# Where six groups of values products of a pair of heads stand in TensorE's order

## The chip, the cores and the metric

The kernel runs on one core of a Trainium2 chip. The metric is the device time of one execution in microseconds (us).

## The reference

Three layers follow each other; only the first is touched. It is attention over 2 x 8 heads of 768 rows and 64 columns in which a query sees a key only if both fall into the same of 16 clusters of their head:

```
q_assign, k_assign = argmax over clusters of normalised q, k against centroids
scores = scale * q @ k.T, masked to q_assign == k_assign
attn = softmax(scores);  attn_out = attn @ v
x = attn_out as 1536 rows of 512
x = sum over 4 experts of p_e * (relu(x @ w1[e]) @ w2[e])
out = leaky_relu(x @ w_in) @ w_out
```

## The kernel before

The 16 heads t = 0 to 15 are worked one after the other, as 8 pairs (an even t and the odd t after it). Every head is cut into six blocks of 128 rows. These are the pieces of work that matter, each with its lines:

- **M(t, j)**, `emit_M`, L509: the scores of one block of queries in a short form, two matmuls (L515) into a 1024-column PSUM tile, and on VectorE (DVE) the largest of each row (L519).
- **E(t, j)**, `emit_E`, L545: the scores of one block of keys against all queries, four matmuls (L550, L551), and on ScalarE (ACT) the exponential of them (L553).
- **P(t, j)**, `emit_P`, L555: the exponentials split into a high f16 part phi (L561 on DVE or L563 on ACT) and a rest plo (L564, on GpSimd, which is POOL, for nearly all).
- **V(t, j)**, `emit_V`, L568: the values products of one block of queries: 18 short f16 matmuls (L576 to L578) of 64 or 65 columns. It reads all of phi and plo of head t and writes the head's own `small` PSUM tile. TensorE (PE) alone works in it. A V group stands about one head behind the E of its head.
- Preparation of a pair to come: transposes T (two per pair, one for q and one for k, L335, split by ACT and DVE, L139 and L140), the similarities simT and sims (L349, L361), the argmax on DVE (L382 to L386), of which L382 and L383 read the sims out of PSUM, and the transpose ohT (L406).
- X of a finished pair: six transposes (L604), split by ACT and DVE (L139, L140). Single transposes mrow (L534) and vall (L458).

M, E, T, simT, sims, ohT, mrow, vall and X take their PSUM tile from one ring of three, `big()` (L126). So each of them can begin only when the reader of the piece that took its tile three pieces earlier is done with it. V takes none of the three.

The order of the work is written out by hand: `at(when, ...)` (L866) gives each piece a place in units of one E, and L959 sorts them by it. `V_AT` (L23) has the places of V(t, 0) to V(t, 5), the first tuple for even heads and the second for odd ones, counted from the start of the following head (L881). Heads 14 and 15 use `V_LAST` instead. Every engine works off its instructions in the order so made.

Of the kernel before, what the change touches and what calls it, by code (L numbers as in the profile page):

```python
# [19 lines left out]
PHI_ON_VECTOR = ((0, 2, 5), (3,))  # L20
PLO_ON_VECTOR = (13, 5)
M_AT = ((1.25, 2.08, 2.35, 3.21, 5.26, 5.79), (0.67, 1.9, 2.06, 2.76, 4.04, 5.42))
V_AT = ((1.84, 2.15, 2.31, 3.56, 4.97, 5.13), (1.44, 2.97, 3.24, 4.31, 4.57, 5.82))  # L23
NORM_AT = (6.53, 6.12)
PREP_V_AT = (2.41, 2.77)
MROW_AT = (1.43, 1.0)
# [49 lines left out]
def attention_moe_kernel(  # L76
# [789 lines left out]
    def at(when, fn, *args):  # L866
        line.append((when, len(line), fn, args))

    for t in range(NH):
# [8 lines left out]
        for j in range(J):  # L878
            if t > 1:
                at(o - 2 * J + M_AT[par][j] if t > 3 else (M2_AT, M3_AT)[t - 2][j], emit_M, t, j)  # L880
            at(o + J + (V_AT if t < NH - 2 else V_LAST)[par][j], emit_V, t, j)  # L881
        at(o + J + (NORM_AT if t < NH - 2 else NORM_LAST)[par], emit_norm, t)
# [551 lines left out]
```

## Time and profile before

| | |
|---|---|
| time, median of 3 (lowest to highest) | 965.48 us (965.24 to 966.52) |
| the profiled execution's own time | 967.07 us |
| its span | 965.4 us |
| PE busy, over the span | 946.0 us (98%) |
| DVE, ACT, POOL busy | 743.8, 518.7, 552.5 us |
| granted TensorE clock | 1.00 |

The attention stage is the first quarter of the span; heads 2 to 13 run from about 59 to 218 us. In the timeline views a row has the start in us, how long the row lasts, the engine, the line, the operation, what is written and read, its shape and how many follow at once. A bracket gives the idle time before it and what ended it. Matmuls overlap each other in these rows, so the time that a piece takes on PE is read as its start to the next piece's start, and a short wait can stand there with no bracket.

### The profile page before, as it was taken

The page shows a single profiled execution, that of the slowest core. Times are in us where ns is not written, and L with a number is a line of the kernel's source. Part 1 is how long each engine was busy: PE and PEld are TensorE (multiplying, and loading weights), DVE is VectorE, ACT ScalarE, POOL GpSimd, SP SyncE. Part 2 cuts the span into 40 slices and gives each one's busy share as a digit, 9 for nine tenths or more (in the row PEclk, how much of TensorE's full clock was granted, in tenths as well). Part 3 has the DMA queues.
Part 4 walks back from the last instruction along what each step waited for, and adds up shares of the span by engine and source line. Part 5 has one row for each costly group of instructions (what it writes and reads, how often), then busy time and mean ns, then how long its engine had stood idle before and what let it go on. Part 6 is the DMA issues. An engine that isn't in the chain of part 4 may idle for free.

```text
span 965.4 us, 16126 instructions
## 1 busy us (share of the span) xinstructions
PE 946.0 (98%) x6339; PEld 545.3 (56%) x6372; DVE 743.8 (77%) x1263; ACT 518.7 (54%) x733; POOL 552.5 (57%) x443
## 2 busy tenths in 40 slices
PE   8899999999999999999999999999999999999998
PEld 5688888887544455555555555555544444444443
DVE  6989998889687766666766666766889997877764
ACT  3677777779434444334344344344486565555642
POOL 4477777780345665455655465654536666676661
PEclk9999999999999999999999999999999999999999
DMA  7775567550111012110211102103101221221003
GB/s 168 181 177 129 127 136 157 118 136 5 44 44 44 23 37 63 44 44 23 66 33 45 44 29 71 44 22 131 68 21 46 87 87 44 88 88 59 29 1 131
DMA packets 59540, 70.80 MB, mean 73 GB/s; under 512 B 25060, under 2 KB 42088, under 8 KB 59464
## 3 DMA queue, kind: packets, MB, share of 16 engines
q1 hardware_dynamic: 59464, 69.77, 26.7%
q8 instruction: 50, 0.82, 0.4%
q14 instruction: 26, 0.21, 0.1%
HBM read 46.19 MB, written 3.17 MB: 51 GB/s over the span
## 4 chain that ended last, share of the span: by engine, by line
PE 78%; DVE 15%; ACT 3%; issue 2%; DMA 1%; POOL 1%; SPq 0%; DVEq 0%; ACTq 0%
PE z L1064 22%; PE z L1194 8%; PE z L1195 7%; PE z L1196 7%; PE z L1075 5%; PE z L1252 4%; PE z L1254 3%; PE z L1253 3%; PE big L515 3%; PE z L1123 3%; DVE m L519 2%; PE big L550 2%; PE big L551 2%; DVE acc L1204 1%; PE small L576 1%
## 5 line engine op out<-in xcount | busy, mean ns | idle before, releaser
L140 POOL TENSOR_TENSOR hlo<-g,hhi 128x512 bf16<-128x512 f32 x140 | 194.4, 1407 | 93.0 <-ACT hhi L139 93.0
L1204 DVE SCALAR_TENSOR_TENSOR acc<-z,outer,acc 128x512 f32<-128x512 f32 x180 | 133.8, 747 | 63.3 <-PE z L1196 63.0
L564 POOL TENSOR_TENSOR plo<-p,phi 128x768 f16<-128x768 f32 x83 | 136.1, 1652 | 72.8 <-ACT phi L563 43.1
L139 ACT ACTIVATE hhi<-g 128x512 f16<-128x512 f32 x140 | 86.8, 628 | 119.3 <-DVE g L797 117.8
L1194 PE MATMUL z<-hhi,w2hi 128*128 128x512 f16 x384 | 145.5, 379 | 1.6
L1195 PE MATMUL z<-hhi,w2lo 128*128 128x512 f16 x384 | 145.5, 379 | 0.0
L267 POOL TENSOR_TENSOR w2lo<-w2raw,w2hi 128x512 f16<-128x512 f32 x46 | 57.2, 1264 | 134.2 <-ACT w2hi L264 134.2
L1196 PE MATMUL z<-hlo,w2hi 128*128 128x512 bf16 x353 | 133.8, 379 | 0.0
L519 DVE TENSOR_REDUCE m<-big 128x1 f32<-128x768 f32 x96 | 89.9, 950 | 13.8 <-PE big L515 13.6
L553 ACT ACTIVATE p<-big 128x768 f32<-128x768 f32 x96 | 76.6, 808 | 33.7 <-PE big L551 28.3
L267 POOL TENSOR_TENSOR w1lo<-w1raw,w1hi 128x512 f16<-128x512 f32 x46 | 55.8, 1234 | 41.6 <-ACT w1hi L264 22.1
L1103 DVE TENSOR_TENSOR part<-z,part 128x512 f32<-128x512 f32 (+1 forms) x62 | 34.8, 578 | 53.9 <-PE z L1064 39.6
L1261 DVE SCALAR_TENSOR_TENSOR accn<-z,outer,accn 128x512 f32<-128x512 f32 x84 | 60.4, 744 | 20.5 <-PE z L1254 20.0
L1075 PE MATMUL z<-xx,w1hi 128*128 128x512 f16 x256 | 76.2, 379 | 0.0
L1252 PE MATMUL z<-w2hi,hhi 128*128 128x512 f16 x192 | 72.8, 379 | 0.1
L1254 PE MATMUL z<-w2hi,hlo 128*128 128x512 f16 x192 | 72.8, 379 | 0.0
L1253 PE MATMUL z<-w2lo,hhi 128*128 128x512 f16 x192 | 72.8, 379 | 0.0
L550 PE MATMUL big<-qka 128*128 128x512 f32 x192 | 70.1, 367 | 2.8 <-DVE m L519 1.2
L797 DVE SCALAR_TENSOR_TENSOR g<-z,pb 128x512 f32<-128x512 f32 x92 | 52.5, 576 | 24.3 <-PE z L1064 10.1
L1064 PEld LDWEIGHTS <-shi 128*128 128x128 f16 x496 | 48.5, 98 | 37.1 <-issue 0.7
L578 PE MATMUL small<-vt,plo 128*128 128x65 f16 x576 | 61.2, 192 | 2.2 <-DVE plo L564 1.6
L1196 PEld LDWEIGHTS <-w2hi 128*128 128x128 f16 x384 | 37.6, 98 | 45.3
(247 smaller groups left out, 2301.5 us busy)
## 6 DMA issues: line engine op xcount, KB each, us to landing
qkb<-pair SPq DMA_DIRECT2D x32, 384.0 KB
w1raw<-in_moe_w_dram SPq DMA_DIRECT2D x16, 512.0 KB
w2raw<-in_moe_w_dram SPq DMA_DIRECT2D x16, 512.0 KB
w1raw<-in_moe_w_in_dram SPq DMA_DIRECT2D x8, 1024.0 KB
w2raw<-in_moe_w_out_dram SPq DMA_DIRECT2D x8, 1024.0 KB
qka<-pair SPq DMA_DIRECT2D x16, 384.0 KB
vraw<-in_v_dram SPq DMA_DIRECT2D x16, 192.0 KB
pb<-pe_rows SPq DMA_DIRECT2D x4, 768.0 KB
```

Source lines behind the costliest of these rows:

```text
L140: lo_engine.tensor_tensor(out=lo, in0=src, in1=as_read(hi), op=ALU.subtract)
L267: nc.gpsimd.tensor_tensor(out=lo[:, x], in0=src[:, x], in1=hi[:, x], op=ALU.subtract)
L519: nc.vector.tensor_reduce(out=m_t[t][:, j:j + 1], in_=ps[:, 0:S], op=ALU.max, axis=AX.X)
L564: (nc.vector if plo_on_vector else nc.gpsimd).tensor_tensor(out=plo, in0=p, in1=phi, op=ALU.subtract)
L1064: nc.tensor.matmul(ps, lhsT=w[i][:, k, :], rhs=x[j][:, k, sub], start=first and k + i + j == 0, stop=k == 1 and i == 1, skip_group_check=True,
L1075: nc.tensor.matmul(like(ps, rhs), lhsT=w[:, k, fs], rhs=rhs, start=k + i == 0, stop=k == KC - 1 and i == 2,)
L1194: nc.tensor.matmul(out, lhsT=whi[:, f, ks], rhs=h, start=f == 0, stop=False)
L1195: nc.tensor.matmul(out, lhsT=wlo[:, f, ks], rhs=h, start=False, stop=False)
L1196: nc.tensor.matmul(out, lhsT=whi[:, f, ks], rhs=l, start=False, stop=f == NF - 1)
L1204: nc.vector.scalar_tensor_tensor(out=a, in0=out, scalar=by, in1=a, op0=ALU.mult, op1=ALU.add)
L1252: nc.tensor.matmul(ps, lhsT=hi[:, f, ts], rhs=whi[:, f, :], start=f == 0, stop=False)
L1253: nc.tensor.matmul(ps, lhsT=hi[:, f, ts], rhs=wlo[:, f, :], start=False, stop=False)
```

## The change

Four numbers of `V_AT` are changed; nothing else is.

```
-V_AT = ((1.84, 2.15, 2.31, 3.56, 4.97, 5.13), (1.44, 2.97, 3.24, 4.31, 4.57, 5.82))
+V_AT = ((2.14, 2.15, 2.31, 3.56, 5.12, 5.13), (1.44, 3.58, 3.59, 4.31, 4.57, 5.82))
```

For heads 0 to 13 this changes the order on PE at three places of a pair. With heads 8 and 9 as the example (pieces on PE only; the ring's tile is taken by all but V):

```
place 1 (even head)
before: sims, E(9,1), mrow, V(8,0), M(11,1), E(9,2), M(11,2), V(8,1), V(8,2), M(11,3)
after:  sims, E(9,1), mrow, M(11,1), E(9,2), M(11,2), V(8,0), V(8,1), V(8,2), M(11,3)
place 2 (even head)
before: E(9,4), M(11,4), X, V(8,4), E(9,5), V(8,5), M(11,5)
after:  E(9,4), M(11,4), X, E(9,5), V(8,4), V(8,5), M(11,5)
place 3 (odd head)
before: E(10,2), M(12,1), M(12,2), V(9,1), E(10,3), M(12,3), T(7,0), V(9,2), T(7,1), E(10,4)
after:  E(10,2), M(12,1), M(12,2), E(10,3), M(12,3), T(7,0), T(7,1), V(9,1), V(9,2), E(10,4)
```

No instruction is added or removed, and no other engine's own order changes, since a V group has none but PE's instructions.

## Rows read from the trace of the kernel before

**Rows 1.** Busy time by stretch, one pair: stretch, length, each engine

```profile
core 0: us, PE busy (x) PEld busy (x) DVE busy (x) ACT busy (x) POOL busy (x), PEclk, DMA share, GB/s
...
168.80:195.60 26.80, 26.38 (x337) 23.10 (x335) 23.75 (x38) 20.97 (x30) 19.69 (x13) 1.00 0.51 112
```

**Rows 2.** Chain of waits, 164 to 172 us: start, us on the chain, engine, tile, line

```profile
167.60 0.96 DVE m L519
...
169.45 1.13 DVE phi L561
...
171.50 0.62 PE big L515 x2
```

**Rows 3.** Timeline of PE around place 1 of heads 8 and 9

```profile
157.75 0.19 PE L576 MATMUL small<-vt,phi 128*128 128x65 f16 x1
...
158.27 0.19 PE L578 MATMUL small<-vt,plo 128*128 128x65 f16 x1
158.47 0.59 PE L515 MATMUL big<-qka 96*128 96x512 f32 x2
158.90 0.40 PE L550 MATMUL big<-qka 128*128 128x512 f32 x1
...
159.61 0.51 PE L515 MATMUL big<-qka 96*128 96x512 f32 x2
159.95 0.21 PE L576 MATMUL small<-vt,phi 128*128 128x65 f16 x1
...
160.51 0.19 PE L576 MATMUL small<-vt,phi 128*128 128x65 f16 x1
```

**Rows 4.** Timeline of PE around place 3 of heads 9 and 10

```profile
172.32 0.20 PE L576 MATMUL small<-vt,phi 128*128 128x65 f16 x1
...
172.88 0.48 PE L550 MATMUL big<-qka 128*128 128x512 f32 x1
...
173.66 0.52 PE L515 MATMUL big<-qka 96*128 96x512 f32 x2
174.03 0.88 PE L335 MATMUL big<-ident,qraw 128*128 128x128 f32 x6
174.74 0.19 PE L576 MATMUL small<-vt,phi 128*128 128x65 f16 x1
...
175.30 0.85 PE L335 MATMUL big<-ident,kraw 128*128 128x128 f32 x6
175.91 0.48 PE L550 MATMUL big<-qka 128*128 128x512 f32 x1
```

**Rows 5.** Timeline of DVE at place 1 of heads 8 and 9

```profile
157.76 0.56 DVE L383 TENSOR_TENSOR eq<-big,mx 128x384 bf16<-128x384 f32 x1
```

**Rows 6.** Timeline of PE, place 1 of heads 4 and 5

```profile
104.53 0.59 PE L515 MATMUL big<-qka 96*128 96x512 f32 x2 [0.32 <-DVE eq L383]
```

**Rows 7.** Line L383, 59 to 245 us: count, ns, first and last start

```profile
L383 DVE TENSOR_TENSOR eq<-big,mx x5: 557/558/559, 76.1 to 184.6; 128x384 bf16<-128x384 f32 x5
```

**Rows 8.** Timeline of DVE, place 1 of heads 12 and 13

```profile
208.48 0.95 DVE L519 TENSOR_REDUCE m<-big 128x1 f32<-128x768 f32 x1
```

**Rows 9.** Timeline of POOL after place 2: plo of block 5 of head 9

```profile
168.51 1.65 POOL L564 TENSOR_TENSOR plo<-p,phi 128x768 f16<-128x768 f32 x1
```

**Rows 10.** Timeline of ACT at place 3: the exponential of E(10, 2)

```profile
171.33 0.81 ACT L553 ACTIVATE p<-big 128x768 f32<-128x768 f32 x1 [0.56 <-PE big L551]
```

**Rows 11.** Timeline of DVE at place 3: the maxima of M(12, 1), M(12, 2)

```profile
172.15 1.82 DVE L519 TENSOR_REDUCE m<-big 128x1 f32<-128x768 f32 x2
```

**Rows 12.** Groups of PE instructions, 59 to 245 us: count, busy us, mean ns

```profile
L335 PE MATMUL big<-ident,qraw 128*128 128x128 f32 x30 | 4.4, 282 | 0.0
```

**Rows 13.** Timeline of DVE, place 3 of heads 11 and 12

```profile
198.97 1.82 DVE L519 TENSOR_REDUCE m<-big 128x1 f32<-128x768 f32 x2
```

**Rows 14.** Timeline of PE at place 2 of heads 8 and 9: X, E(9, 5)

```profile
164.42 0.82 PE L604 MATMUL big<-ident,xn 128*128 128x128 f32 x6
...
165.63 0.48 PE L550 MATMUL big<-qka 128*128 128x512 f32 x1
```

**Rows 15.** Timeline of ACT at place 2: the exponential of E(9, 4)

```profile
164.33 0.81 ACT L553 ACTIVATE p<-big 128x768 f32<-128x768 f32 x1 [0.19 <-PE big L551]
```

## The prediction

> **What bounds the kernel now.** I read the page first, then the busy time by stretch, then the timeline of PE, and for every short wait of PE the timeline of the engine that ends it. In the attention stage a pair of heads takes about 26.8 us, of which PE is busy for 26.38; DVE has 23.75, ACT 20.97 and POOL 19.69, and the granted clock is 1.00 throughout [rows 1]. So what a pair costs is PE's own work plus a few waits that hardly show. The chain of waits says where they lie: it runs along PE except at one point of a pair, where it goes from a row maximum over the conversion to phi and the next maximum to the M that waited for its PSUM tile [rows 2]. Two more waits stand in the timeline with no bracket, and the change touches both.
>
> **What a join can save.** An E that follows an M takes 0.71 us to the next piece (158.90 to 159.61) [rows 3]; one that follows a V group takes 0.78 (172.88 to 173.66) [rows 4]. An M after V takes 0.43 (158.47 to 158.90), after E 0.34 (159.61 to 159.95) [rows 3]. So each passage from short f16 matmuls back to f32 ones costs 0.07 to 0.09 us. Three passages a pair over seven pairs would be 21 x 0.08 = 1.7 us. At place 2 nothing of it is real: X is a run of short transposes too, and there E follows X where it followed V, with the same passage bounded by 0 and 0.09.
>
> The Trainium skill (TensorE: Matmul & The Clock Gate, Architectural detail: the array is 16× 32×32, not 1× 128×128) says that TensorE's queue can pull a weight load ahead of matmuls that still run. By that rule the passage is free, and a join saves 0 instead of 1.7 us; the rows above, 0.78 against 0.71, do not agree with it in full.
>
> **Place 1.** V(8,0) runs from 157.75, its last matmul starts at 158.27, and M(11,1) starts at 158.47 [rows 3]. A V group takes 0.56 (159.95 to 160.51) [rows 3], so PE was free at 158.31 and waited 0.16. The reason: the ring gives M(11,1) the tile of sims, three pieces earlier, and sims is read last by L383 on DVE, which ends at 157.76 + 0.56 = 158.32 [rows 5]. For heads 4 and 5 the view names this releaser itself, with 0.32 of idle PE [rows 6]. So V(8,0) is what PE does while DVE still holds the tile. After the change PE comes to M(11,1) at 157.75, and the tile is still not free before 158.47, since nothing that L383 waits for has moved: 0.72 us of idle PE. M(11,1), E(9,2) and M(11,2) then run as before, and V(8,0) is added ahead of V(8,1). M(11,3) starts a whole V group later: +0.56, at most +0.59 if M's own first load is no longer behind the V, and no less than +0.48 if the passage saved by the join is all kept. I take 0.56. Behind the waiting M stand E(9,2) and all later PE work; V matmuls cannot step past it.
>
> L383 is there five times, from 76.1 to 184.6 us, for heads 2, 4, 6, 8 and 10 [rows 7]. For head 12 there are no sims, and the ring gives M(15,1) the tile of M(15,0), whose maximum ends at 208.48 + 0.95 = 209.43 [rows 8]; the same wait. Six times 0.56 = 3.4 us. Head 0 lies among the waits of the start: between 0 and 0.56, I take 0.2.
>
> Does the delay reach the end? From M(11,3) to X PE has no wait, so X comes 0.56 later; ACT's split of X, phi of block 4, then plo on POOL follow in order, and POOL's last plo ends at 168.51 + 1.65 = 170.16 [rows 9], just before the conversion that the chain passes at 169.45 + 1.13 = 170.58 [rows 2]. Both ways, over POOL and over the maxima, begin behind the added group, so M(12,1) at 171.50 moves by the same amount.
>
> **Place 3.** V(9,1) runs from 172.32 to 172.88, then E(10,3), M(12,3) at 173.66, and T(7,0) at 174.03 [rows 4]. After the change E(10,3) comes at 172.32; its tile was E(10,2)'s, read by ACT until 171.33 + 0.81 = 172.14 [rows 10], so it need not wait. M(12,3) would come at 172.32 + 0.71 = 173.03, but takes the tile of M(12,1), and T(7,0) that of M(12,2). Both maxima stand as one row on DVE, 172.15 + 1.82 = 173.97 [rows 11]. M(12,1)'s half ends near 173.1; M(12,2)'s ends at 173.97, 0.06 before T(7,0) started. So T(7,0) cannot come sooner than 174.03: the 0.56 of V(9,1) and the 0.07 of the passage turn into idle PE. T(7,0) takes 0.71 (174.03 to 174.74) and T(7,1) 0.61 (175.30 to 175.91) [rows 4]; a T straight after a T stands nowhere, and I bound it by 0.61 and 0.71. Then V(9,1), V(9,2) at 0.56 each. E(10,4) comes at 174.03 + 0.71 + 0.61 to 0.71 + 1.12 = 176.47 to 176.57, against 175.91: +0.56 to +0.66. I take 0.56, a V group, as at place 1. T(7,1) does come earlier, by 0.56, but its split on ACT and DVE is waited for by nobody near.
>
> The q transposes count 30 in this stretch, six to a head: five heads, 1, 3, 5, 7 and 9 [rows 12]; 5 x 0.56 = 2.8 us. Head 11 has no T; M(14,3) then waits for the first half of 198.97 + 1.82 [rows 13], about the 0.07 to 0.13 that is left after the join: 0.1. Head 13 has no M and no T there: 0 to -0.08, I take 0. From E(10,4) to the next maximum wait PE is without waits, so this too goes through.
>
> **Place 2.** X takes 164.42 to about 165.08; E(9,5) would come then instead of at 165.63 [rows 14]. Its tile is E(9,4)'s, read until 164.33 + 0.81 = 165.14 [rows 15]: 0.06 to 0.12 of wait, and up to 0.09 for the passage. So M(11,5) comes 0 to 0.2 later. The conversion that follows ends only behind POOL's 170.16 [rows 9], which does not depend on place 2; I take 0, and 6 x 0.2 = 1.2 us if that cover is not there.
>
> **Sum.** 3.4 + 0.2 + 2.8 + 0.1 + 0 = 6.5 us. The profiled execution took 967.07 us (span 965.4, and 1.7 around it); it would become 973.6. The median of the runs is 965.48, 1.6 lower; the same 6.5 on it gives 972.0.
>
> **Rivals.** (a) The tiles come free earlier than I read them: the 0.16 before M(11,1) has no bracket, and T(7,0) shows no wait at all. Then all three joins keep their passage: 965.48 - 1.7 = 963.8, not slower. It decides if L383 releases before 157.75, or M(12,2)'s maximum before 173.4. Against it: both starts follow the DVE rows by 0.15 and 0.06, and the row of heads 4 and 5 names L383 [rows 6]. By the rule of the Trainium skill cited above (a) would come to 965.5. (b) Place 1 is absorbed: M(12,1) waited for DVE in any case [rows 2], and if that wait hangs on something older than X, the later PE only uses it up. 965.48 + 6.5 - 3.4 = 969.1 or, with head 0, 968.9. Against it: everything on that chain I could follow begins behind the added V. (c) Place 2 is not covered either: 972.0 + 1.2 = 973.2. For it: the chain view puts the maximum of M(11,5) on its way [rows 2].
>
> **Chances.** The forecast, both places pay: 0.66, with 970.5 to 973 of its own; (c) 0.10; (b) 0.12; (a) 0.12, of which a third is faster by over 0.2%, and two thirds are within it. About 0.2% (1.9 us) is what a measurement of this kernel can tell from no change. Slower 0.88, same 0.08, faster 0.04. The range goes from 968.0, under (b), to 974.0, over (c); it leaves out (a) and some of the rest.
>
> **What would show it.** After the change: M(11,1) (first of two L515 behind the single L534) with about 0.7 us of idle PE that DVE's L383 ends, in five pairs, and for head 12 one that L519 ends; T(7,0) with some 0.4 us that L519 ends; the pair at 27.9 instead of 26.8 us, with PE's busy time unchanged or a little lower, and the feed-forward part as long as before. If M(11,1) comes within 0.2 us behind mrow, place 1 was misread; if T(7,0) starts under 0.2 us behind M(12,3)'s end, place 3 was. If both idle times are there and the pair is not longer, the delay was taken back behind M(12,1) or in the last two heads, and the sum is wrong in what reaches the end.

## The result, and the profile after

The changed kernel takes 971.92 us (median of 6 runs, 971.19 to 973.18) against 965.36 for the kernel before beside it (6 runs, 965.17 to 966.66): ratio 1.0063 [1.0053, 1.0074], slower, and 0.1 us from the forecast. That closeness is partly luck: executions of either kernel differ by up to 2 us in their start-up (E(1,0) starts between 42.4 and 44.3 us in the traces), and three of the six runs of after, against two of the six of before, are over 1 us longer than the rest. So from here on I compare by place: how much later a PE instruction starts than in the kernel before, counted from the start of E(1,0), which stands ahead of every changed place. For this the two ends of the attention stage, of PE's timeline before and after:

```profile
44.33 0.40 PE L550 MATMUL big<-qka 128*128 128x512 f32 x1
...
247.87 0.82 PE L604 MATMUL big<-ident,xn 128*128 128x128 f32 x6
```

```profile
42.45 0.40 PE L550 MATMUL big<-qka 128*128 128x512 f32 x1
...
252.01 0.82 PE L604 MATMUL big<-ident,xn 128*128 128x128 f32 x6
```

From E(1,0) to X(7) it is 203.54 us before and 209.56 after: the attention stage is 6.0 us longer. The shortest runs of the two, 971.19 and 965.17, lie as far apart. The profiled execution of after started 1.88 us earlier in this count, and took 971.24 us where the one of before took 967.07: 4.17, which is 6.02 - 1.88 within 0.03. The feed-forward part behind it is as long as it was: 717.5 us from X(7) to the end of the span in both.

The stretch of one pair, which answers to [rows 1] (stretch, length, busy time of each engine):

```profile
core 0: us, PE busy (x) PEld busy (x) DVE busy (x) ACT busy (x) POOL busy (x), PEclk, DMA share, GB/s
171.22:199.20 27.98, 26.87 (x337) 23.02 (x335) 23.23 (x38) 21.14 (x30) 19.76 (x13) 1.00 0.49 108
```

The pair went from 26.80 to 27.98, with the same 337 matmuls and the same clock. PE's busy time rose by 0.49, though it does nothing more: this is waiting that the profile draws as work. Two rows below show it. The single L534 is drawn 0.27 long, and the M behind it came 0.03 later where its tile was free (e5 below); M(12,3) is drawn 0.62 long, and took 0.37 before.

PE around place 1 of heads 8 and 9, as [rows 3], and DVE there, as [rows 5]:

```profile
159.36 0.27 PE L534 MATMUL big<-ident,m 128*6 128x128 f32 x1
160.20 0.59 PE L515 MATMUL big<-qka 96*128 96x512 f32 x2 [0.56 <-DVE eq L383]
...
161.33 0.51 PE L515 MATMUL big<-qka 96*128 96x512 f32 x2
161.69 0.21 PE L576 MATMUL small<-vt,phi 128*128 128x65 f16 x1
...
162.80 0.19 PE L576 MATMUL small<-vt,phi 128*128 128x65 f16 x1
```

```profile
159.49 0.56 DVE L383 TENSOR_TENSOR eq<-big,mx 128x384 bf16<-128x384 f32 x1
```

L383 ends at 160.05, and M(11,1) starts 0.15 behind it: the same 0.15 as before, but now with nothing between L534 and M(11,1). Then come E(9,2), M(11,2) and three V groups in a row (161.69 to 163.35) instead of two.

PE around place 3 of heads 9 and 10, as [rows 4], and DVE there, as [rows 11]:

```profile
174.61 0.50 PE L550 MATMUL big<-qka 128*128 128x512 f32 x1
...
175.46 0.62 PE L515 MATMUL big<-qka 96*128 96x512 f32 x2
176.32 0.88 PE L335 MATMUL big<-ident,qraw 128*128 128x128 f32 x6 [0.25 <-DVE m L519]
177.03 0.82 PE L335 MATMUL big<-ident,kraw 128*128 128x128 f32 x6
177.69 0.19 PE L576 MATMUL small<-vt,phi 128*128 128x65 f16 x1
...
178.78 0.48 PE L550 MATMUL big<-qka 128*128 128x512 f32 x1
```

```profile
174.44 1.82 DVE L519 TENSOR_REDUCE m<-big 128x1 f32<-128x768 f32 x2
```

The two maxima end at 176.26 and T(7,0) starts 0.06 behind them, as before. E(10,3) and M(12,3) are ready earlier and gain nothing by it.

What PE waits for over the attention stage (releaser, us in total, times, longest):

```profile
PE big L515 <- DVE eq L383: 3.0, 5, 0.7
PE big L335 <- DVE m L519: 1.2, 5, 0.3
...
PE big L515 <- DVE m L519: 1.1, 1, 1.1
```

Five waits of M for L383, one for L519 (M(15,1), head 12) and five of T for L519. Before, L383 ended one such wait, 0.3 long [rows 6], and no T waited visibly. The chain of waits after (start, us, what), of which [rows 2] showed a part, now leaves PE at both places:

```profile
159.49 0.57 DVE eq L383
...
160.20 0.59 PE big L515 x2
...
174.51 1.76 DVE m L519 x2
...
176.32 0.77 PE big L335 x5
```

### The profile page after: what moved, and what is told of

Read it like the earlier page. It is cut to its first block, busy times and chain, and to the rows that moved or that the text cites. A ratio compares the mean times of both kernels' runs of the same rounds, so it can differ in the third digit from the quotient of the medians.

```text
span 969.5 us, 16159 instructions
## 1 busy us (share of the span) xinstructions
PE 948.0 (98%) x6372; PEld 543.3 (56%) x6372; DVE 740.9 (76%) x1263; ACT 519.1 (54%) x733; POOL 552.7 (57%) x443
## 4 chain that ended last, share of the span: by engine, by line
PE 76%; DVE 17%; ACT 2%; issue 2%; DMA 2%; POOL 1%; SPq 0%; DVEq 0%; ACTq 0%
PE z L1064 22%; PE z L1196 8%; PE z L1195 8%; PE z L1194 8%; PE z L1075 5%; DVE m L519 4%; PE z L1252 3%; PE z L1254 3%; PE z L1253 3%; PE z L1123 3%; PE big L515 2%; PE big L550 2%; PE big L551 1%; PE small L576 1%; PE small L577 1%
## 5 line engine op out<-in xcount | busy, mean ns | idle before, releaser
L139 ACT ACTIVATE hhi<-g 128x512 f16<-128x512 f32 x140 | 86.7, 628 | 119.4 <-DVE g L797 117.8
L1196 PE MATMUL z<-hlo,w2hi 128*128 128x512 bf16 x384 | 145.6, 379 | 0.0
L519 DVE TENSOR_REDUCE m<-big 128x1 f32<-128x768 f32 x96 | 90.0, 952 | 22.0 <-PE big L515 21.8
L1196 PEld LDWEIGHTS <-w2hi 128*128 128x128 f16 x384 | 37.6, 98 | 45.3
L1194 PEld LDWEIGHTS <-w2hi 128*128 128x128 f16 x384 | 37.6, 98 | 43.7
```

The source lines that it names most:

```text
L519: nc.vector.tensor_reduce(out=m_t[t][:, j:j + 1], in_=ps[:, 0:S], op=ALU.max, axis=AX.X)
L1194: nc.tensor.matmul(out, lhsT=whi[:, f, ks], rhs=h, start=f == 0, stop=False)
L1196: nc.tensor.matmul(out, lhsT=whi[:, f, ks], rhs=l, start=False, stop=f == NF - 1)
```

## The experiments

**One place at a time.** Three kernels, each with one third of the change. Place 1 alone:

```
-V_AT = ((1.84, 2.15, ...
+V_AT = ((2.14, 2.15, ...
```

> Place 1 alone is joined (V(t,0) of even heads goes behind M(t+3,2)); places 2 and 3 stand as in the kernel before. Theory (the moved group was what PE did while DVE still held the ring's tile): M(11,1) starts as late after sims as before, with some 0.55 us of idle PE that L383 ends, M(11,3) 0.56 later in each of heads 2 to 12, 0.36 at head 0: +3.7 us over the stage. Rival (it is the join of places, or a delay that spreads, that costs): under a half of the whole +6.0. Rival (a) of the prediction: -0.5.

Measured: 969.68 us (968.86 to 970.87), ratio 1.0045 [1.0029, 1.0062]; by place +3.63. The steps stand at M(5,3), M(7,3) ... M(15,3), 0.53 to 0.58 each, and 0.29 at head 0. PE at M(11,1), with its wait:

```profile
158.53 0.58 PE L515 MATMUL big<-qka 96*128 96x512 f32 x2 [0.57 <-DVE eq L383]
```

Place 3 alone:

```
-... (1.44, 2.97, 3.24, 4.31, 4.57, 5.82))
+... (1.44, 3.58, 3.59, 4.31, 4.57, 5.82))
```

> Place 3 alone is joined (V(t,1) and V(t,2) of odd heads go behind both transposes). Theory: T(7,0) starts 0.06 us behind the maximum of M(12,2) as before, with 0.25 us of idle PE in the view and as much again hidden before it, E(10,4) 0.58 later in heads 3, 5, 7 and 9, about 0.5 at head 1, 0 at heads 11 and 13: +2.8 us. Rival: the groups cost this only together with place 1: under +1.5.

Measured: 967.64 us (967.58 to 969.25), ratio 1.0021 [1.0012, 1.0031]; by place +2.39. Five steps of 0.59 and one of 0.17 (head 11) make 3.1, but 0.70 comes back between heads 3 and 5. ACT, DVE and POOL there, first of the kernel before, then of e3:

```profile
94.55 0.81 ACT L139 ACTIVATE pair<-big 128x768 fp32r<-128x768 f32 x1 [0.43 <-PE big L335]
```

```profile
98.61 0.88 DVE L737 TENSOR_SCALAR ds<-ds 128x12 f32<-128x12 f32 x1
```

```profile
96.17 3.29 POOL L564 TENSOR_TENSOR plo<-p,phi 128x768 f16<-128x768 f32 x2 [1.03 <-ACT phi L563]
```

```profile
92.08 1.51 ACT L139 ACTIVATE pair<-big 128x768 fp32r<-128x768 f32 x2 [0.86 <-PE big L335]
```

```profile
97.97 0.17 DVE L737 TENSOR_SCALAR ds<-ds 128x12 f32<-128x12 f32 x1
```

```profile
96.44 1.65 POOL L564 TENSOR_TENSOR plo<-p,phi 128x768 f16<-128x768 f32 x1 [0.39 <-ACT phi L563]
```

L737, a step of the expert shares on 12 columns, ends right behind POOL's plo in both: 99.49 behind 99.46, and 98.14 behind 98.09. L737 starts 1.65 behind M(6,4) in each of these kernels, but POOL's work does not keep its place. Where place 3 is joined (e3, and after), the second transpose, T(4,1), starts 4.43 ahead of M(6,4) instead of 3.29. ACT then splits both transposes without a break (the L139 rows), the phi behind them starts 1.1 earlier, and POOL's last plo ends 0.12 behind L737's start instead of 0.85. So L737 takes 0.17 instead of 0.88. DVE is what the sims and the pieces behind them, up to M(7,1), wait for just there, so about 0.7 is won. Place 1 alone does not move T(4,1): in e1 L737 takes 0.87 again (97.57 to 98.44, POOL until 98.41), and nothing comes back. That E(4,3) comes earlier too is not what does it: in e6 and e7 further down E(4,3) comes 0.7 earlier against M(6,4) and T(4,1) does not, and there L737 takes 0.88 and 0.91 and nothing comes back. Three runs at the end test that it is L737.

Place 2 alone:

```
-V_AT = ((1.84, 2.15, 2.31, 3.56, 4.97, 5.13), ...
+V_AT = ((1.84, 2.15, 2.31, 3.56, 5.12, 5.13), ...
```

> Place 2 alone is joined (V(t,4) of even heads goes behind E(t+1,5)). Theory: M(11,5) comes about 0.15 us later, E(9,5) waits for the exponential of E(9,4), and M(12,1) takes it back, since the conversion ahead of its release ends behind POOL: 0 to +0.1 us over the stage, with the idle PE before M(12,1) at 0.13 instead of 0.27. Rival (c): the chain view is right that the maximum of M(11,5) sets M(12,1): +0.9 us, and the idle time before M(12,1) stays at 0.27.

Measured: 965.45 us (965.14 to 967.14), ratio 1.0001 [0.9991, 1.0010]; by place +0.10. PE at M(12,1), before and in e2:

```profile
171.50 0.86 PE L515 MATMUL big<-qka 96*128 96x512 f32 x3 [0.27 <-DVE m L519]
```

```profile
169.79 0.85 PE L515 MATMUL big<-qka 96*128 96x512 f32 x3
```

M(11,5) comes 0.14 later and M(12,1) not at all: between the end of the row ahead of it and M(12,1) lie 0.14 instead of 0.27, too little for a bracket. Rival (c) falls. Even the +0.10 is hardly place 2's. Up to M(9,1), each M(t,1) is within 0.03 of its place; then, once in this trace, M(10,0) waits 0.72 us for a DMA (qka<-ohT), and 0.12 of it stays. The three parts sum to 3.63 + 2.39 + 0.10 = 6.12, or 6.0 without that wait, against 6.02 for all: they hardly touch each other.

**What holds the tile at place 1.** In the changed kernel a head's normalisation stands on DVE ahead of L382 and L383. Here it is put behind them:

```
-NORM_AT = (6.53, 6.12)
+NORM_AT = (6.53, 6.75)
```

> The changed kernel with one more edit: the normalisation of odd heads (three DVE instructions, about 1 us) goes from ahead of the maximum of M(t+4,0) to behind L383. DVE's total work is the same, but L383 ends about 0.97 us earlier. Theory: M(11,1) finds its tile free and its 0.56 us of idle PE go; so does the wait of M(15,1) for M(15,0): about -3.4 us against the changed kernel, +2.6 to +2.8 against the kernel before (places 3 and the start stay). Rival (the joined order costs in itself, not by the wait for L383): no change against the changed kernel.

Measured: 970.84 us (970.78 to 972.45), ratio 1.0057 [1.0042, 1.0072]; 0.47 less than after by place, where 3.4 was expected. A miss. DVE and PE there:

```profile
158.58 0.56 DVE L382 TENSOR_REDUCE mx<-big 128x24 f32<-128x384 f32 x1 [0.33 <-PE big L361]
159.17 0.56 DVE L383 TENSOR_TENSOR eq<-big,mx 128x384 bf16<-128x384 f32 x1
```

```profile
157.09 1.45 PE L361 MATMUL big<-both,simT 128*128 128x64 f32 x12
158.35 0.48 PE L550 MATMUL big<-qka 128*128 128x512 f32 x1
...
159.13 0.27 PE L534 MATMUL big<-ident,m 128*6 128x128 f32 x1
159.88 0.59 PE L515 MATMUL big<-qka 96*128 96x512 f32 x2 [0.47 <-DVE r L589]
```

L382 now waits for the sims themselves: L383 starts 2.08 behind the first L361, where it was 2.16 in after, so that it comes 0.08 earlier and not 0.97. From E(9,1), right behind L361, to M(11,1) it is 159.88 - 158.35 = 1.53 us, the time of two DVE instructions and their hand-overs; E(9,1) and L534 fill at most 0.89 of it (158.35 to 159.13, and 0.11). (The view names L589 only because it started last before the M; L383 ends at 159.73, 0.15 ahead as ever.) So the order on DVE matters little: PE simply has too little other work between writing this tile and wanting it back, and V(8,0) was that work.

**The tile given back early.** The changed kernel with the sims of pairs 3 and later copied to SBUF by ACT, so that L382 and L383 read the copy:

```
+        kept = prep.tile([128, J * 4 * C], F32, tag="simsk", ...)
+        nc.scalar.activation(out=kept, in_=ps[:, 0:J * 4 * C], func=AF.Copy)
```

> The changed kernel, but for pairs 3 to 7 ACT copies the sims out of PSUM into a buffer in SBUF and DVE reads them there, so that the ring's tile is free after ACT's copy and not after L383. The order on PE is that of the changed kernel. Theory (M(11,1) waits for its tile, not for its place in the order): the 0.56 us of idle PE before it goes in five pairs, down to under 0.1: -2.8 us against the changed kernel, and place 1 then costs about 0 against the kernel before; head 12, which has no sims, keeps its wait. Rival (the joined order costs in itself): no change. A side effect that could hide it: L383 with two operands in SBUF may take longer beside POOL.

Measured: 979.33 us (978.61 to 980.06), ratio 1.0140 [1.0126, 1.0153]; 7.4 more than after, where 2.8 less was expected. A miss in time, though not in what it took away. PE, ACT and DVE there (lines past 363 are 5 higher):

```profile
165.15 0.27 PE L539 MATMUL big<-ident,m 128*6 128x128 f32 x1
165.18 0.59 PE L520 MATMUL big<-qka 96*128 96x512 f32 x2
166.57 0.50 PE L555 MATMUL big<-qka 128*128 128x512 f32 x1 [0.80 <-ACT p L558]
```

```profile
164.60 0.49 ACT L368 ACTIVATE simsk<-big 128x384 f32<-128x384 f32 x1 [0.77 <-PE big L361]
164.99 0.83 ACT L568 ACTIVATE phi<-p 128x768 f16<-128x768 f32 x1
165.72 0.80 ACT L558 ACTIVATE p<-big 128x768 f32<-128x768 f32 x1
```

```profile
166.30 1.69 DVE L389 TENSOR_TENSOR eq<-eq,first 128x384 bf16<-128x384 bf16 x1
...
170.11 1.71 DVE L391 TENSOR_TENSOR oh<-eq,mb 128x384 bf16<-128x384 bf16 x1
```

M(11,1) comes 0.03 behind L539: the tile alone had held it. But the next piece, E(9,2), wants the tile of E(9,1), and its exponential on ACT, now behind the copy and a phi, ends at 166.52. There is a second wall right behind the first. In the kernel before that exponential ended at 157.90 + 0.81 = 158.71, 0.19 ahead of E(9,2) at 158.90 [rows 3], and in after at 160.43, 0.20 ahead of it. So even without the copy little would be won by freeing the first tile alone: by my estimate from these rows 0.15, the 0.20 less a hand-over of 0.05. The rest of the loss is on DVE: L389 and L391 took 1.7 us where they take 0.82 and 0.55 in after, both beside POOL's plo (165.95 to 169.50, 169.76 to 171.41), and PE waited 5.9 us in five pairs for L391.

**The same pieces, with the cover left.** Is it the joining that costs, or the wait laid bare? Two kernels on the one before move V(9,1) behind E(10,3) and M(12,3), but ahead of T(7,0), where it still covers the maximum of M(12,2); the second also brings V(9,2) there, so that the groups are joined. (T's own place is named 3.22 instead of 3.21 to let the V's stand ahead of it; what else has a place keeps its order.)

```
e6: -... 2.97,  3.24, ...   +... 3.213, 3.24,  ...
e7: -... 2.97,  3.24, ...   +... 3.212, 3.214, ...
both: -T_AT = (3.21, 3.57)  +T_AT = (3.22, 3.57)
```

> The kernel before with V(t,1) of odd heads moved as far as the changed kernel moves it past E and M, but set ahead of the first transpose instead of behind both: M(12,2), E(10,3), M(12,3), V(9,1), T(7,0), V(9,2), T(7,1), E(10,4). Theory (place 3 costs because nothing stands ahead of T(7,0) while the maxima of M(12,1) and M(12,2) run): no idle PE before T(7,0), E(10,4) as in the kernel before, -0.1 to +0.1 us a pair, 0 to +0.5 us in all. Rival (moving V(9,1) past E and M costs in itself): +0.5 a pair, +2.4 in all.

> The kernel before with the same two groups of odd heads joined, but ahead of both transposes: M(12,2), E(10,3), M(12,3), V(9,1), V(9,2), T(7,0), T(7,1), E(10,4). Theory (it is the uncovered wait, not the join): no idle PE before T(7,0), E(10,4) within 0.1 us of the kernel before, -0.5 to +0.5 us in all, against +2.4 of the join behind the transposes. Rival (joined groups cost by themselves): +2.4.

Measured: e6 966.14 us (966.04 to 967.84), ratio 1.0005 [0.9996, 1.0014], by place +0.84; e7 966.03 us (965.97 to 967.42), ratio 1.0003 [0.9994, 1.0012], by place +0.77. PE and DVE in e7:

```profile
171.78 0.61 PE L515 MATMUL big<-qka 96*128 96x512 f32 x2
172.24 0.21 PE L576 MATMUL small<-vt,phi 128*128 128x65 f16 x1
...
173.36 0.85 PE L335 MATMUL big<-ident,qraw 128*128 128x128 f32 x6
```

```profile
170.77 0.96 DVE L519 TENSOR_REDUCE m<-big 128x1 f32<-128x768 f32 x1
```

Neither wins anything, but with V ahead of T there is no idle time before T(7,0), and a step of 0.59 becomes one of 0.10 to 0.14 (0.17 at head 11, as in e3): 0.8 in all, against 3.1, or 2.39 with what came back. What is lost is the cover, not the separation. The rest that is still lost reads the same way, though no run took it away: V(9,1) stood ahead of M(12,3) too, which takes the tile of M(12,1). In the kernel before, that maximum ends 0.55 ahead of M(12,3). In e3, e6 and e7 M(12,3) starts 0.05 to 0.06 behind its end (in e7 171.78 behind 170.77 + 0.96), a wait with no bracket, at head 11 as well.

**More cover at place 1.** On the kernel before, V(8,1) is put beside V(8,0), ahead of M(11,1), to fill the 0.16 that PE still waited there:

```
-V_AT = ((1.84, 2.15, ...
+V_AT = ((1.84, 1.85, ...
```

> The kernel before with V(t,1) of even heads moved the other way, ahead of M(t+3,1): sims, E(9,1), mrow, V(8,0), V(8,1), M(11,1), E(9,2), M(11,2), V(8,2), M(11,3). Theory (a V group ahead of M(11,1) covers the wait for L383, and 0.16 of that wait is left in the kernel before): that rest goes in heads 2 to 10, M(11,3) comes 0.16 earlier: -0.6 to -1.0 us in all, if DVE does not take it back at the argmax. Rival (V groups cost the same wherever they stand): 0.

Measured: 965.53 us (965.43 to 967.20), ratio 1.0000 [0.9991, 1.0009]; by place +0.23. A miss. PE and DVE:

```profile
157.44 0.19 PE L576 MATMUL small<-vt,phi 128*128 128x65 f16 x1
...
158.54 0.60 PE L515 MATMUL big<-qka 96*128 96x512 f32 x2
...
161.98 0.52 PE L406 MATMUL big<-identb,oh 128*64 128x128 bf16 x6
```

```profile
161.37 0.55 DVE L386 TENSOR_TENSOR oh<-eq,mb 128x384 bf16<-128x384 bf16 x1
```

Two groups fill 157.44 to 158.54, the wait is gone and M(11,3) comes 0.15 sooner in its pair. But L406, which needs L386, starts 0.06 behind it, and is 0.16 later: it takes the gain back. The +0.23 is made elsewhere: +0.54 at head 0, of which 0.3 comes back at heads 4 and 5. DVE's row of steps from the sims to L386 sets the pace there; filling a gap of PE that lies inside it wins nothing.

**What came back at heads 3 to 5.** Three kernels take L737 off DVE: e9 leaves it out of the kernel before, e10 puts it on ACT there, e11 does that in the changed kernel:

```
-        nc.vector.tensor_scalar(out=ds, in0=ds, scalar1=1e-9, scalar2=None, op0=ALU.add)
+        nc.scalar.activation(out=ds, in_=ds, func=AF.Copy, bias=1e-9)
```

> The kernel before without L737, the sum of 1e-9 to the expert shares' divisors on DVE; this addition is left out of what is computed. In the kernel before L737 takes 0.88 us (98.61 to 99.49) while POOL's plo runs until 99.46; in place 3 alone it takes 0.17 with POOL done early. Theory: it is this instruction that stands behind POOL, so without it L738 starts at about 98.61 and still takes 0.23; DVE's next maximum ends 0.9 earlier, and as PE waits for DVE there (M(7,0) 0.74 instead of 0.36, the sims, M(7,1) 0.32), M(7,3) comes 0.7 to 0.9 us earlier: about 964.6. Rival: any short DVE instruction in that place stands behind POOL; then L738 takes about 0.9 instead of 0.23, and 0 to 0.2 us are won.

> The kernel before with L737 on ACT instead of DVE, nothing left out. ACT is idle from 98.37 to 98.91 there. Theory (POOL holds up L737 on DVE alone): the addition runs on ACT at about 98.65 for 0.2 us, L738 starts near 98.9 instead of 99.53, and M(7,3) comes 0.5 to 0.65 us earlier: about 964.8, at the edge of what can be told from no change. Rival: nothing is won (0 to 0.1), since L738 stands behind POOL in its place, or ACT's copy of simT (98.91) is pushed back.

> The changed kernel with L737 on ACT. There L737 takes 0.17 on DVE, since POOL's plo is done in time. Theory: the 0.70 that came back between heads 3 and 5 is this same instruction's, so moving it now wins nothing, and the way over ACT costs 0 to 0.15 us: about 971.3 by its lower group of runs (971.2), M(7,3) 0 to 0.15 later. Rival (the 0.70 came from something else): M(7,3) comes 0.5 us or more earlier here as well.

Measured: e9 964.86 us (964.68 to 967.05), ratio 0.9997 [0.9988, 1.0006], M(7,3) 0.49 earlier; e10 964.86 us (964.68 to 966.59), ratio 0.9998 [0.9990, 1.0007], M(7,3) 0.51 earlier; e11 971.34 us (971.26 to 972.70), ratio 1.0064 [1.0050, 1.0078], M(7,3) at 0.01 of its place in after. So the 0.7 was this instruction's: on the kernel before it can be won in part, on the changed kernel there is nothing left to win. e10 and e11 came out as expected; e9 won less than the 0.7 to 0.9 expected. DVE and POOL of e9:

```profile
96.81 0.23 DVE L738 RECIPROCAL ds<-ds 128x12 f32<-128x12 f32 x1
97.07 0.65 DVE L739 TENSOR_TENSOR dp<-dp,ds 128x48 f32<-128x48 f32 x1
```

```profile
94.37 3.27 POOL L564 TENSOR_TENSOR plo<-p,phi 128x768 f16<-128x768 f32 x2 [1.04 <-ACT phi L563]
```

The reciprocal runs through beside POOL at its usual 0.23; the product behind it takes 0.65 where it took 0.21, and ends at 97.72, 0.08 behind POOL's 97.64. Which instruction stands behind POOL depends on its form and on when it comes. e10 is the one version that computes all that the kernel before does and is ahead of it: by 0.53 us by place, and by as much between the shortest runs (964.68 against 965.21), but that is too little for the interval.

## Why the prediction was right, point by point

- **Place 1, 3.4 + 0.2 for head 0.** Right in mechanism and size: 3.63 alone (e1). The M came 0.81 late (160.20, against 159.36 + 0.03 with a free tile), where I had 0.72; the row shows only 0.56 of it as idle.
- **Place 3, 2.8 + 0.1.** Right in mechanism, mis-sized in terms of opposite sign, of which the larger was put at nothing. A step is 0.59, not 0.56: T(7,1) straight behind T(7,0) takes 0.66 (177.03 to 177.69), in the middle of my bounds, and I had taken the lower end. Head 11 gave 0.17, not 0.1. Against that, 0.70 came back at heads 3 to 5, which I had not seen: I wrote that the split of the second transpose, which comes earlier, "is waited for by nobody near", but at heads 3 to 5 a phi, POOL's plo and L737 on DVE stand behind it. I also assumed that the later PE work goes through everywhere, and took [rows 6], whose 0.32 was a sign that DVE was late in that pair, only to name the releaser. e3 alone measured 2.39 for a forecast of 2.9.
- **Place 2, 0.** Right, with the 0 to 0.2 at M(11,5) measured as 0.14, and the cover shown by the wait of M(12,1), 0.27 to 0.14.
- **The passages.** No join shows its saving. M(11,1) takes 0.43 after its wait, as it took behind V, and E(10,3) behind M takes 0.85 (174.61 to 175.46), since M(12,3) then waits. At both paying places PE only arrives earlier at a tile that is not free. At place 2 the bound was at its zero end: E(9,5) behind X takes 0.81, as behind V. Where the change touches nothing, the rows stand as I read them: E about 0.70 behind M with an M or an E next, about 0.78 behind V. So the rule of the Trainium skill that I weighed (TensorE: Matmul & The Clock Gate, Architectural detail: the array is 16× 32×32, not 1× 128×128), that a weight load can be pulled ahead of running matmuls, does not make these passages free: the 0.08 is still there, what it consists of no run shows, and for the sum it did not matter.
- **The rivals.** (a) falls with the eleven waits named above. (b) falls as it was put, since M(12,1) came 4.17 later in its place, all that PE had gathered at the places before but for place 2's 0.14; a small form of it, at one pair and of another origin, is the 0.70. My sum for (b) was wrong: 965.48 + 6.5 - 3.4 is 968.6, and 968.4 without head 0's 0.2, not 969.1 and 968.9; the range takes in both. (c) falls with e2.
- **The sum.** 6.5 predicted, 6.0 by place; the 0.5 that the medians show on top goes with the spread of start-up, and that it brings the time to the forecast is luck. Of the signs that I named, PE's unchanged busy time did not hold: part of the new wait is drawn as busy, so that the idle times show as 0.56 and 0.25 and not as 0.7 and 0.4.

## What to carry to other kernels

A short piece between two others may be there for what it covers: before moving it, look up which buffer the next piece takes over, who reads that buffer last, and when that reader ends against the time at which the engine would now arrive. If the reader ends later by the length of the piece, the whole piece goes onto the path, once per turn of the loop, and a saved passage only lengthens the wait. The row to look for need not have an idle mark in the kernel before: a start that follows another engine's end by a constant short time, here 0.06 or 0.15 us, is the sign.

## What the runs showed of the hardware

- From the end of the last reader of a PSUM tile to the start of the waiting matmul it was 0.06 us behind DVE's row maximum and 0.05 behind ACT's exponential (166.52 to 166.57 in e5), but 0.15 behind L383, the same in before, after and e4.
- Beside POOL's 128x768 instruction some DVE instructions stand until it ends: L737 on 12 columns 0.88 us instead of 0.17, L739 on 48 columns 0.65 instead of 0.21 (0.41 in e10), each ending 0.03 to 0.08 us behind POOL. L738, a reciprocal, did not. The Trainium skill (SBUF — State Buffer, SBUF: two separate sides) says that DVE in a two-port mode or with two SBUF inputs, and GpSimd, take one pair of ports in turn, each for its whole instruction. These rows agree with it, though no row shows in which mode L737 ran, and no run took POOL's own work away.
- Matmul rows in front of a wait were drawn up to 0.25 us too long: the 0.81 us ahead of M(11,1) showed as 0.56, and the 0.16 that it waited in the kernel before had no idle mark.
